# The loads of a and V begun from ScalarE's queue instead of SyncE's, in a Mamba-2 scan followed by a low-rank mixer

## The chip, the cores and the metric

The kernel runs on one core of one Trainium2 chip. The metric is the device time of one execution in microseconds (us). The engines of the core are named as the profile names them: PE (TensorE; PEld are its weight loads), DVE (VectorE), ACT (ScalarE), POOL (GpSimd) and SP (SyncE); SPq is the queue of SP, from which loads and stores are begun.

## The reference

Two blocks follow each other. The first is a chunked state-space scan over 4 batches, 8 heads, 768 steps, with head dimension 32 and state dimension 16; the second mixes its output along the sequence with two low-rank factors U and V and along the channels with two weight matrices.

```python
log_a = np.log(np.clip(a, 1e-06, 1.0))
for c in range(nc):                      # chunks of 32 steps
    cum = np.cumsum(la, axis=-1)
    L = np.exp(cum[:, :, :, None] - cum[:, :, None, :]) * causal
    CB = np.einsum('bhin,bhjn->bhij', Cc, Bc)
    y_intra = np.einsum('bhij,bhjd->bhid', CB * L, xc)
    y_inter = np.einsum('bhin,bhnd->bhid', Cc, state) * decay_to_i[:, :, :, None]
    y[:, :, sl] = y_intra + y_inter
    state = decay_full[:, :, None, None] * state + np.sum(Bx, axis=2)
...
h = xt @ U @ V                           # xt: (batch, 256, 768); U: 768 x 32; V: 32 x 768
u = x + h.transpose(0, 2, 1)
ch = np.maximum(u @ w_ch1, 0.0) @ w_ch2
return (u + ch).astype(np.float32)
```

U, V and the two weights come as 64-bit numbers and are turned into 32-bit ones on the chip from their integer words.

## The kernel before

The sequence is worked in blocks of 256 steps: 4 batches times 3 blocks make 12 pairs, numbered 0 to 11. For each pair the kernel loads x, B and C, scales B and C by the decays (tile BC), transposes them on PE (tiles T and Cm), forms the masked products (tile M), adds up the state (tiles S and Sm), and sums the outputs in PSUM (yT). For each batch the mixer then multiplies by U and V and by the weights.

The order of all work is written out by hand, as one list of words called PLAN. A word's first letters name a step and its numbers say on what: `A` the decays, `Q` the scaling of B and C, `V1.1.2` a transposition (not the load of V), `g` and `m`/`M` the products and their masks, `n` and `j` the two halves of the output inside a chunk, `s` and `u` the state, `y` the copy of yT, `c` and `C` the conversions of words, `v` the spreading of V over the partitions, `F` idle products on PE that are put ahead of the next step, `p`/`q`/`a` the low-rank part, `f`/`e`/`h`/`d`/`U` the channel part. Every engine works through its own instructions in the order of the list.

Loads are words too. `B`, `X` and `w` are held until the last DVE instruction ahead of them in the list is done. With a `Y` in front a load is begun as soon as its turn comes in SP's queue; with a `Z` in front it is begun from ACT's queue instead. No word of the list of before has a `Z`. `follow` picks the queue:

```python
if name[0] in "YZ":
    issuer[0] = nc.scalar if name[0] == "Z" else nc.sync
    early[name[1]](*at)
    issuer[0] = nc.sync
```

SP's queue therefore begins, in this order: a (ahead of the list, L186), U, B and C of pair 0, x of pair 0, pair 1, the B and C of pair 2, the four loads of V (`YV0`), the first half of the first weights (`w0`, held until `Q2.0`), x of pair 2, B and C of pair 3, and so on; L202 is the line of `begin`, through which all loads but a's go. The four loads of V bring one quarter of V's columns each to 32 partitions (48 KB each).

The first steps are these. ACT begins with the load of its function table (L182). PE runs idle products from the moment its identity matrix is there (L136), then transposes a (L343); DVE clips the result, ACT takes the logarithm (L349), and all decays come from that. V is needed by the conversion `C0`, and then by `v0`, which makes Vn (L880) and Vs (L890).

Of the kernel before, what the change touches and what calls it, by code (L numbers as in the profile page):

```python
# [32 lines left out]

PLAN = (
# [39 lines left out]
def kernel(  # L74
# [27 lines left out]
    nc = tc.nc  # L102
# [60 lines left out]
    class Kept:  # L163
# [6 lines left out]
        def __getattr__(self, name):  # L170
# [8 lines left out]
    vector = Kept(nc.vector)  # L179
    until = []  # L180

    nc.scalar.preload_act_table_set("natural_log_exp_and_others")  # L182


    a_sb = const.tile([NB * NH * NC // 2, 2, P], FP32)
    nc.sync.dma_start(  # L186
        out=a_sb,
        in_=a.rearrange("(g b) h (c s) -> g (b h c) s", g=2, s=P).rearrange(
            "g r s -> r g s"))

    x_sb, bc_sb = {}, {}
    pairs = [(b, q) for b in range(NB) for q in range(NPR)]
# [68 lines left out]
    U2, V2, w12, w22 = (w.bitcast(INT32) for w in (moe_U, moe_V, moe_w_ch1, moe_w_ch2))  # L261
# [721 lines left out]
```

## Time and profile before

| | |
|---|---|
| median of 3 runs | 224.49 us (224.32 to 224.66) |
| the profiled execution | 224.41 us |
| its span in the profile | 222.6 us |
| PE busy | 215.5 us, 97% of the span |
| DVE, ACT, POOL busy | 146.4, 108.7, 32.7 us |
| granted clock of PE | 0.999 |
| load of a, issue to landing | 2.0 us |
| loads of V, issue to landing | 2.8 us (median of four) |

The profile tells of one execution. A line of the timeline gives start, duration, engine, source line, operation, what is written from what, how often, and in brackets the idle time before it with what ended it. A line of the chain gives start, duration, engine, tile and source line of one piece of the chain of work that ended last.

### The profile page before, as it was taken

How to read it: one execution, taken by the hardware profiler on the slowest of the kernel's cores; microseconds unless marked ns; L12 is line 12 of the kernel's file. 1: busy time of each engine (PE TensorE's matmuls, PEld its weight loads, DVE VectorE, ACT ScalarE, POOL GpSimd, SP SyncE). 2: the span in 40 equal slices, each digit the busy share in tenths (PEclk: the TensorE clock that was granted, in tenths of full speed). 3: DMA queues.
4: the chain of work that ended last, by engine and by line, in shares of the span. 5: the costliest groups of instructions: out<-in, count | busy, mean ns of one | idle time of the engine just before them, and what ended most of it. 6: DMA issues, size and time to landing. Idle time of an engine off the chain costs nothing.

```text
span 222.6 us, 7025 instructions
## 1 busy us (share of the span) xinstructions
PE 215.5 (97%) x3022; PEld 182.2 (82%) x3022; DVE 146.4 (66%) x314; ACT 108.7 (49%) x251; POOL 32.7 (15%) x44
## 2 busy tenths in 40 slices
PE   7999999999999999999999999999999999999994
PEld 4666566665668888889999996788999999999993
DVE  4688498568657755737955736959863955674921
ACT  3334745675668075543444214476535455553510
POOL 3012223405577053000010100000000000000000
PEclk9999999999999999999999999999999999999999
DMA  6968888898633446100120010000000100101011
GB/s 102 129 98 144 138 158 189 187 281 113 134 47 71 84 57 91 37 24 28 27 71 27 3 49 27 3 3 3 0 27 1 47 0 27 47 0 50 6 43 50
DMA packets 69520, 14.59 MB, mean 66 GB/s; under 512 B 63792, under 2 KB 67696, under 8 KB 69488
## 3 DMA queue, kind: packets, MB, share of 16 engines
q1 hardware_dynamic: 69488, 14.13, 32.3%
q8 instruction: 24, 0.39, 0.8%
q14 instruction: 8, 0.07, 0.1%
HBM read 10.98 MB, written 3.15 MB: 63 GB/s over the span
## 4 chain that ended last, share of the span: by engine, by line
PE 89%; DVE 5%; DMA 2%; SPq 2%; ACT 1%; issue 1%; POOL 0%; POOLq 0%
PE x L790 31%; PE z L790 24%; PE y L790 12%; PE y L680 3%; PE x L522 2%; PE y L642 2%; PE w L482 2%; DMA bc<-in_B_dram 2%; DVE M L174 2%; PE w L707 2%; SPq L202 2%; PE w L556 1%; PE x L136 1%; PE z L522 1%; PE w L734 1%; PE w L136 1%
## 5 line engine op out<-in xcount | busy, mean ns | idle before, releaser
L790 PE MATMUL z<-u,w 128*128 128x384 f32 x144 | 33.6, 347 | 0.0
L790 PE MATMUL x<-u,w 128*128 128x384 f32 x144 | 32.7, 344 | 0.5 <-DVE u L174 0.3
L174 DVE SCALAR_TENSOR_TENSOR words<-words 128x768 fp32r<-128x768 f32 (+3 forms) x35 | 29.5, 846 | 1.4
L790 PEld LDWEIGHTS x<-u,w 128*128 128x128 f32 x144 | 24.8, 188 | 1.8 <-DVE u L174 0.7
L795 ACT ACTIVATE x<-x 128x384 f32<-128x384 f32 (+1 forms) x30 | 13.6, 454 | 25.1 <-PE x L790 18.2
L790 PEld LDWEIGHTS z<-u,w 128*128 128x128 f32 x144 | 24.1, 189 | 0.9
L790 PE MATMUL x<-w2c,words 128*128 128x256 f32 x112 | 22.3, 339 | 0.0
L795 ACT ACTIVATE z<-z 128x384 f32<-128x384 f32 (+1 forms) x27 | 12.6, 466 | 18.6 <-PE z L790 18.6
L790 PE MATMUL y<-w,words 128*128 128x256 f32 x144 | 19.8, 283 | 0.0
L790 PEld LDWEIGHTS x<-w2c,words 128*128 128x128 f32 x112 | 18.3, 189 | 1.5
L174 DVE SCALAR_TENSOR_TENSOR words<-x,words 128x384 fp32r<-128x384 f32 x24 | 13.3, 554 | 9.3 <-ACT words L825 9.2
L790 PEld LDWEIGHTS y<-w,words 128*128 128x128 f32 x144 | 18.8, 190 | 0.3
L583 POOL TENSOR_TENSOR Sm<-S,own 128x256 f32<-128x256 f32 (+1 forms) x12 | 7.6, 634 | 76.4 <-DVE S L174 48.0
L174 DVE SCALAR_TENSOR_TENSOR words<-z,words 128x384 fp32r<-128x384 f32 x24 | 13.2, 552 | 5.2 <-ACT words L825 5.1
L825 ACT ACTIVATE words<-z 128x384 fp32r<-128x384 f32 x24 | 11.7, 491 | 10.1 <-PE z L790 10.0
L825 ACT ACTIVATE words<-x 128x384 fp32r<-128x384 f32 x24 | 11.8, 493 | 5.3 <-PE x L790 5.0
L790 PE MATMUL x<-w,words 128*128 128x256 f32 x96 | 14.2, 285 | 0.0
L790 PEld LDWEIGHTS x<-w,words 128*128 128x128 f32 x96 | 12.9, 190 | 0.2
L680 PEld LDWEIGHTS y<-M,x 64*32 64x32 f32 x768 | 8.1, 105 | 5.7 <-issue 3.0
L174 DVE TENSOR_TENSOR BC<-bc,F 128x512 f32<-128x512 f32 (+2 forms) x18 | 9.4, 535 | 4.7 <-DMA bc<-in_B_dram 3.2
L680 PE MATMUL y<-M,x 64*32 64x64 f32 x768 | 12.0, 223 | 0.4 <-DVE settled L174 0.3
L174 DVE SCALAR_TENSOR_TENSOR S<-S,kept,w 128x64 f32<-128x64 f32 x40 | 11.2, 279 | 1.6
(149 smaller groups left out, 411.9 us busy)
## 6 DMA issues: line engine op xcount, KB each, us to landing
words<-in_moe_w_ch_dram SPq DMA_DIRECT2D x7, 512.0 KB, 5.0
x<-in_x_dram SPq DMA_DIRECT2D x24, 128.0 KB, 3.7
out_dram<-ytok SPq DMA_DIRECT2D x24, 128.0 KB, 1.7
bc<-in_B_dram SPq DMA_DIRECT2D x24, 64.0 KB, 3.3
bc<-in_C_dram SPq DMA_DIRECT2D x12, 128.0 KB, 3.4
words<-in_moe_w_ch_dram SPq DMA_DIRECT2D x2, 256.0 KB, 3.8
words<-in_moe_U_dram SPq DMA_DIRECT2D x1, 192.0 KB, 2.9
words<-in_moe_V_dram SPq DMA_DIRECT2D x4, 48.0 KB, 2.8
```

Source lines behind the costliest of these rows:

```text
L136: nc.tensor.matmul(out=t[:, :m * P].rearrange("p (m i) -> p m i", i=P), lhsT=ident, rhs=ident[:, None, :].to_broadcast([P, m, P]), start=T ...
L174: self.last = call(*args, **kwargs)
L202: op = issuer[0].dma_start(**kwargs)
L482: nc.tensor.transpose(out=tp[:, i, v], in_=s["BC"][:, i, c + v].rearrange("p h n -> p (h n)"), identity=ident)
L522: nc.tensor.matmul(out=s["g"][r][cols, c], lhsT=s["T"][rows, 0, c, cols], rhs=s["Cm"][rows, :, :, ts(2 * c + p, Q)].rearrange("r v t i -> ...
L583: nc.gpsimd.tensor_tensor(out=s["Sm"][:, sl], in0=s["S"][:, sl].rearrange("p i (s d) -> p i s d", s=2), in1=own2[:, b, 4 * q + sl.start:4 ...
L642: behind["first"].append(nc.tensor.matmul(out=channels(k)[r // 2][ts(r % 2, H), c, p], lhsT=own[ts(r, Q)], rhs=st[k]["T"][ts(r, Q), 1, :, ...
L680: product = nc.tensor.matmul(out=y[n][ts(i, Q), c, p], lhsT=x_sb[k][half, c, h], rhs=s["M"][half, h // 2, c, h % 2], start=fresh(k, n, [i] ...
L707: nc.tensor.transpose(out=t[:, c, g], in_=yT[b][:, g, ts(2 * q + c, P)], identity=ident)
L790: nc.tensor.matmul(out=t, lhsT=lhsT, rhs=rhs, start=start, stop=True, skip_group_check=True)
L795: nc.scalar.activation(t, t, AF.Copy, scale=1.0 + EPS)
L825: nc.scalar.activation(gs[j, m // 2][0][:, m % 2], t, AF.Relu, scale=NEAR)
```

## The change

The load of a is begun from ACT's queue, and the load of ACT's function table, which came first, now comes behind it. The word `YV0` becomes `ZV0`: V's four loads are begun from ACT's queue, at the place in ACT's order that the word has in the list, behind the two activations of `V1.1.2` and ahead of the copy of `V2.0.2`. Nothing else is changed.

```diff
-    'm0 Q1.1 V1.1.2 M0 u0 YX1 F5 F3 n0 YB2 g1 m1 YV0 Q2.0 w0 Q2.2 YX2 s1 i0 F3 V2.0.2 M1 j0 Q2.1 u1 '
+    'm0 Q1.1 V1.1.2 M0 u0 YX1 F5 F3 n0 YB2 g1 m1 ZV0 Q2.0 w0 Q2.2 YX2 s1 i0 F3 V2.0.2 M1 j0 Q2.1 u1 '
...
-    nc.scalar.preload_act_table_set("natural_log_exp_and_others")
-
-
     a_sb = const.tile([NB * NH * NC // 2, 2, P], FP32)
-    nc.sync.dma_start(
+    nc.scalar.dma_start(
         out=a_sb,
         in_=a.rearrange("(g b) h (c s) -> g (b h c) s", g=2, s=P).rearrange(
             "g r s -> r g s"))
+
+    nc.scalar.preload_act_table_set("natural_log_exp_and_others")
```

## The prediction

> **What bounds the kernel now.** I read the page first: span 222.6 us, the profiled run's own time 224.41, so 1.81 us lie outside the span; TensorE (PE) is busy 97%. By stages, PE is busy 22.11 us of the first 25 and 193.36 of the remaining 197.60, so a load can matter in the first 25 us only, or through a shift that these hand on to the end. Then I read the chain that ended last, in order of time, in that stage:
>
> ```profile
> 1.43 1.65 PE x L136 x2
> 3.08 0.33 PE w L343 x2
> ...
> 15.56 0.34 DVE M L174
> 15.90 0.04 SPq L202
> ...
> 15.99 1.39 SPq L202
> ...
> 19.61 4.09 DMA bc<-in_B_dram
> ...
> 23.72 0.69 DVE BC L174
> 24.41 0.10 DVE settled L174
> ...
> 24.55 0.46 PE y L680 x32
> ```
>
> Up to 15.9 us it is PE and VectorE (DVE); then it goes over SyncE's queue (SPq) and the load of pair 3's B, which ends at 23.7. This reads as if SP's queue were the limit. Whether it is depends on how much room the compute path beside it has, so next the timelines of SP, ACT, PEld (weight loads), DVE and PE, around the places of the change:
>
> ```profile
> 0.80 1.28 ACT L182 ACT_TABLE_LOAD   x1 [0.80 <-PEq L967]
> 0.81 0.38 SPq L186 DMA_DIRECT2D a_sb<-in_a_dram  x1
> 1.24 0.44 SPq L202 DMA_DIRECT2D words<-in_moe_U_dram  x1
> 2.82 0.29 PEld L343 LDWEIGHTS w<-ident,a_sb 96*128 96x128 f32 x2 [0.89 <-DMA a_sb<-in_a_dram]
> 2.88 0.37 PE L343 MATMUL w<-ident,a_sb 96*128 96x96 f32 x1
> 12.73 0.63 ACT L492 ACTIVATE Cm<-x,slot 128x128 f32<-128x128 f32 x2
> 13.46 1.98 SPq L202 DMA_DIRECT2D words<-in_moe_V_dram  x4
> 15.56 0.38 SPq L202 DMA_DIRECT2D words<-in_moe_w_ch_dram  x1
> 16.34 0.37 ACT L486 COPY T<-x 128x256 f32<-128x256 f32 x1 [2.98 <-PE x L482]
> 20.52 0.32 PE L556 MATMUL w<-x,BC 64*32 64x64 f32 x8 [0.26 <-DMA x<-in_x_dram]
> 21.07 0.35 PE L886 MATMUL y<-Vn,ident 32*32 32x192 f32 x2 [0.23 <-ACT Vn L880]
> 24.35 0.15 DVE L174 COPY settled<-slot 128x1 f32<-128x1 f32 x1
> 24.55 0.46 PE L680 MATMUL y<-M,x 64*32 64x64 f32 x32 [0.34 <-DVE settled L174]
> ```
>
> To be seen: a lands just as PE wants it; ACT sits idle for 2.98 us where V's loads are to go; and only two PE waits of the stage, 0.26 and 0.34 us, are ended by loads.
>
> **1. a, from SP to ACT.** Removed from SP: one issue; U begins at 0.81 in place of 1.24, and everything behind it moves up 0.43 us. Added to ACT: an issue of about the same 0.38 us, at 0.80, ahead of the table load. The table load then runs from about 1.2 to 2.5; the first activation that needs it starts at 3.98, so 1.5 us of cover hide it (gone, the cover would cost what the load overshoots, at most 0.4).
> The price is where a lands. Before, a (192 packets, 12 for each of the 16 DMA engines) has these engines nearly alone: between 1.80 and 2.35 us they move 193 packets at a 59.9% share, 27 ns each, 0.33 us an engine. U (768 packets, 48 an engine) follows: 430 packets between 2.5 and 3.0 at 94.8%, 17.6 ns each, 0.84 us an engine. After, both start at 0.8. If the engines take the two queues packet by packet, a's 12 packets have up to 12 of U's between them, 12 x 17.6 = 0.21 us; a little less, since U's packets came 1.13 us after its issue and a's 1.03. Bounds: 0 (a keeps its place ahead) and 0.84 (all of U goes first). Earlier it can hardly land, since both engines' first instructions start at 0.80 to 0.81; and earlier would bring nothing: the 384-column warm-up passes run 0.64 us apart further on (the two at L136 from 3.68 to 4.96), and the second one here, from 2.235, is through at 2.875, exactly when L343's first matmul starts. So a has 0.05 us of room (weight load at 2.82, matmul at 2.88). I take 0.18 later, the value of the interleaving, near the low bound because a's packets start about 0.1 ahead: 0.18 - 0.05 = +0.13 us for L343. Behind it PE works through fills in fixed order to 9.15, and DVE, PE and DVE in turn to 15.9, without a wait on a load: the 0.13 goes on.
> The trace of before has one load queue, so no row shows two at once. [...]
>
> **2. V, from SP to ACT.** Removed from SP: four issues, 1.98 us from 13.46 to 15.44. But SP's next load, w0, is held until the DVE product Q2.0 is done; that is the first of the two BC products of 14.94 and is finished at 15.2, set by PE and DVE. So w0 starts at 15.3 instead of 15.56, and SP gains 0.26, not 1.98. What follows (X2, B3, B5 and so on) comes 0.26 us earlier at least, up to some 0.6 when V's bytes are already out of the way.
> Added to ACT: four issues of 0.42 to 0.58, 1.85 us with their gaps taken as on SP, behind the two Cm activations (12.73 to 13.36) and ahead of the T copy of 16.34. 13.36 + 1.85 = 15.2, so 1.1 us of the 2.98 idle are left: nothing. What is queued behind them is that T copy, then the Cm's and the yT copies of 17.12; PE waits for each of them (L680 at 17.57 starts as yT is done). [...] V lands at 18.2 before, and DVE's first V conversion starts at 18.39 right behind the Cm of 17.68; earlier landing moves nothing.
>
> **3. What the earlier SP queue is worth.** Two PE waits. (a) 0.26 at 20.52 for X2's second half. With it gone PE is through with L556 earlier, and then stands longer at 21.07, for Vn: ACT makes Vn at 20.65 to 21.01 behind the yT copies of 20.11, which PE's own L680 releases. Worth 0. (b) 0.34 at 24.55 for "settled". This tiny DVE copy also has to wait for the 32 products of L680 at 23.76, the last of which ends at 24.22, and its semaphore comes at 24.32; the BC product that the load held up frees DVE at about 24.33. The two are level, so the load gives 0.02 us at most. The same at 28.64: DVE was held 0.32 us by a load at 27.50, but the M product there needs PE's L522, ending 28.58. Worth 0 to 0.04. I take -0.03 for all three.
> [...]
>
> **Sum.** 0.13 - 0.03 = +0.10 us on the profiled 224.41, so 224.51; the median of the three runs is 224.49, so about 224.6.
>
> **Rivals.**
> - Faster: the compute path has more room than the rows let me see (a level pair is a matter of hundredths, and inferred releasers can name the wrong one), and both waits fall away: -0.26 - 0.34 = -0.60, a not later: 223.9. For it: the chain as the profile draws it does run over SP and B3. Against: (a) and (b) above.
> - Slower, U ahead of a: with 0.84 us of U's packets in front, a lands 0.84 later, minus the 0.05 of room: +0.79, and all of it reaches the end: 225.3. It decides from a landing 0.5 us late, at about 3.3, on. For it: SP's and ACT's first issue start within 0.01 us. Against: half-way interleaving is likelier.
> - Slower, ACT held: if V's issues take over 0.745 us each (2.98 / 4), the T copy starts late; at 1.0 each (X2's first issue took 1.39), 1.0 us late: 225.5.
> - The move does nothing: ACT's issues serve in the same order as SP's did, a lands at 2.78: 224.5.
>
> **How the numbers follow.** A measurement of this kernel can tell about 0.2%, 0.45 us, from no change. Forecast (a later by up to 0.5, rest hidden) 0.54, nothing 0.04: together 0.58 within. U ahead of a 0.19, ACT held 0.08: 0.27 slower. Waits fall away 0.15: faster. The range runs from the faster rival to U ahead of a: 223.8 to 225.3; the forecast's own part is 224.4 to 224.9.
>
> **What would show it.** Right: L343's first weight load at 2.9 to 3.1; U's landing, 4.15 before, near 3.8; V's four issues on ACT done before 16.3 and the T copy not later than PE's L482; w0 at 15.3; PE's 0.26 at 20.52 gone and the 0.23 at 21.07 grown; "settled" at 24.3 to 24.6. Wrong: L343 at 2.82 with a shorter span (rival one), L343 after 3.3, or ACT's T copy behind V's issues.

## The result: 1.1 us slower, and the profile after

The changed kernel takes 225.49 us (median of 5 runs, 225.25 to 226.01) against 224.35 for the kernel before, measured beside it (5 runs, 223.81 to 224.66). The ratio over all runs is 1.0066, with a 95% interval of 1.0051 to 1.0080, which is 1.1 to 1.8 us; that of the medians alone, 1.0051, stands at the lower end. The profiled execution took 225.49 us, its span is 223.8.

The chain that ended last now starts with a load. The columns are start, duration, engine, tile and line (the lines of the new kernel are one lower than those of the old):

```profile
0.80 3.15 DMA a_sb<-in_a_dram
3.95 0.05 issue
4.00 0.58 PE w L342 x2
4.58 0.48 PE x L136 x2
...
21.93 0.26 ACT Vn L879
...
25.52 0.17 DVE settled L174
...
```

a takes 3.15 us from issue to landing, where it took 1.97; it lands at 3.95 instead of 2.78, and PE transposes it at 4.00 instead of 2.88. From there on the chain is PE, ACT and DVE only. SP and the load of pair 3's B, which stood in the chain before, are out of it. The timelines of ACT, SP, PEld and PE show the places of the change:

```profile
0.80 0.45 ACTq L183 DMA_DIRECT2D a_sb<-in_a_dram  x1
1.28 1.28 ACT L188 ACT_TABLE_LOAD   x1 [1.28 <-PEq L966]
0.81 0.43 SPq L201 DMA_DIRECT2D words<-in_moe_U_dram  x1
4.00 0.29 PEld L342 LDWEIGHTS w<-ident,a_sb 96*128 96x128 f32 x2 [2.07 <-DMA a_sb<-in_a_dram]
13.64 0.32 ACTq L201 DMA_DIRECT2D words<-in_moe_V_dram  x1
14.01 0.43 ACTq L201 DMA_DIRECT2D words<-in_moe_V_dram  x1
14.47 0.91 ACTq L201 DMA_DIRECT2D words<-in_moe_V_dram  x2
16.42 0.37 SPq L201 DMA_DIRECT2D words<-in_moe_w_ch_dram  x1
17.51 0.37 ACT L485 COPY T<-x 128x256 f32<-128x256 f32 x1 [2.98 <-PE x L481]
22.23 0.35 PE L885 MATMUL y<-Vn,ident 32*32 32x192 f32 x2 [0.57 <-ACT Vn L879]
25.73 0.46 PE L679 MATMUL y<-M,x 64*32 64x64 f32 x32 [0.34 <-DVE settled L174]
```

The shift is 1.12 us at a's transposition (4.00 against 2.88), 1.17 at ACT's T copy (17.51 against 16.34), 1.18 at the "settled" product (25.73 against 24.55), 1.2 over the span, and 1.14 in the medians. Between these two profiles it arises in one place and is handed on whole. The medians are less exact than that: against the 29 runs of before that stand beside the first experiments (224.16) the loss would be 1.33.

In the packets of the trace a's delay has three parts. Its first packet comes at 2.24 instead of 1.84 (0.41 later), although a was issued at the same moment. Its 192 packets take 0.96 us from the first to the last instead of 0.59 (0.37 more). And from the last packet to the landing 0.75 us pass instead of 0.36 (0.39 more). Together that is 1.17. The packets of the two loads are mixed: of U's 768, 190 start ahead of a's first, 500 between a's first and last and 78 behind; 227 packets of B of pair 0 lie there too.

### The profile page after: what moved, and what is told of

It reads as the page before. It is cut to its first block, busy times and chain, and to the rows that moved or that the text cites. A ratio compares the mean times of both kernels' runs of the same rounds, so it can differ in the third digit from the quotient of the medians.

```text
span 223.8 us, 7025 instructions
## 1 busy us (share of the span) xinstructions
PE 215.6 (96%) x3022; PEld 182.1 (81%) x3022; DVE 146.2 (65%) x314; ACT 108.6 (49%) x251; POOL 32.4 (14%) x44
## 3 DMA queue, kind: packets, MB, share of 16 engines
HBM read 10.98 MB, written 3.15 MB: 63 GB/s over the span
## 4 chain that ended last, share of the span: by engine, by line
PE 93%; DVE 3%; DMA 1%; ACT 1%; issue 0%
PE x L789 31%; PE z L789 24%; PE y L789 12%; PE y L679 4%; PE y L641 3%; PE x L521 3%; PE w L481 2%; PE w L706 2%; PE w L555 2%; DMA a_sb<-in_a_dram 1%; PE x L136 1%; PE z L521 1%; PE w L733 1%; PE w L751 1%; PE x L761 1%; PE w L741 1%
## 5 line engine op out<-in xcount | busy, mean ns | idle before, releaser
L824 ACT ACTIVATE words<-z 128x384 fp32r<-128x384 f32 x24 | 11.7, 490 | 10.2 <-PE z L789 10.0
```

Of the source, the lines that this page charges most:

```text
L824: nc.scalar.activation(gs[j, m // 2][0][:, m % 2], t, AF.Relu, scale=NEAR)
```

## The experiments

The theory (S): a's landing beside SP's first load is the whole difference. The rivals: V's loads on ACT cost or bring something (V); ACT's queue, or the table load behind a, is slow by itself (Q). The runs of before beside them have a median of 224.16 (29 runs) for V alone, a alone, U held back and the reverse, and of 224.13 (14 runs) for the other three.

**V alone on ACT's queue.**

```diff
-... g1 m1 YV0 Q2.0 w0 ...
+... g1 m1 ZV0 Q2.0 w0 ...
```

> Only V's four loads go to ACT's queue; a stays on SP, ahead of U. Theory S (the 1.1 us come from a's landing beside U's packets): a lands at 2.78 as before, L343's first weight load at 2.82, and the time is that of before, 224.35 within 0.3; w0 starts near 15.3, PE's 0.26 wait at 20.5 is gone and the wait for Vn has grown to about 0.5. Theory V (V's issues on ACT cost, or the earlier SP queue gives, part of it): the time differs from before by over 0.3 us, up (ACT's T copy of 16.34 late) or down.

Measured: 224.33 us (12 runs), ratio 1.0004 (0.9993 to 1.0014). Timelines of its SP, ACT and PE:

```profile
14.61 0.37 SPq L202 DMA_DIRECT2D words<-in_moe_w_ch_dram  x1
15.70 0.37 ACT L486 COPY T<-x 128x256 f32<-128x256 f32 x1 [2.98 <-PE x L482]
20.42 0.35 PE L886 MATMUL y<-Vn,ident 32*32 32x192 f32 x2 [0.41 <-ACT Vn L880]
23.86 0.46 PE L680 MATMUL y<-M,x 64*32 64x64 f32 x32 [0.34 <-DVE settled L174]
```

ACT still waits 2.98 us for PE ahead of the T copy, w0 is begun right behind Q2.0, the wait for X2 is gone, the wait for Vn has grown from 0.23 to 0.41, and the 0.34 at "settled" stands. V's move is worth nothing that these runs can tell, and the interval leaves it 0.3 us at most, so theory V falls. (This execution ran some 0.65 us ahead of that of before from 12 us on; the last section says why.)

**a alone on ACT's queue.**

```diff
-    nc.scalar.preload_act_table_set(...)
-    nc.sync.dma_start(out=a_sb, ...)
+    nc.scalar.dma_start(out=a_sb, ...)
+    nc.scalar.preload_act_table_set(...)
```

> Only a goes to ACT's queue, ahead of the table load; V stays on SP. Theory S: a lands at 3.95 as in the changed kernel, 1.1 to 1.2 us slower than before, 225.5. Theory V: less than the whole difference, since V's share is missing.

Measured: 225.44 us (4 runs), ratio 1.0061 (1.0042 to 1.0081); a lands at 3.97:

```profile
0.80 3.17 DMA a_sb<-in_a_dram
```

That is the time of the changed kernel within 0.05 us, so the whole loss is a's.

**U held back, a on ACT.** The changed kernel, but SP's first load waits for a short DVE instruction.

```diff
+    begun = vector.memset(ref, 0.0)
...
+            if name == "YU":
+                until[:] = [begun]
```

> The changed kernel, but U (SP's first load) is held until DVE's memset of ref is done, so that it starts at about 1.25 us, as it did behind a on SP; a is still on ACT, ahead of the table load. Theory S: a's packets have the DMA engines to themselves again, a lands at 2.75 to 2.9, and the time goes back to that of before, 224.4 within 0.3. Theory Q (ACT's queue itself, or its first load, or the moved table load is slow): a still lands at 3.3 or later, and the time stays at 225.0 or above.

Measured: 224.33 us (12 runs), ratio 1.0004 (0.9993 to 1.0015). Timelines of its ACT, SP and PEld:

```profile
0.80 0.39 ACTq L183 DMA_DIRECT2D a_sb<-in_a_dram  x1
1.24 0.42 SPq L201 DMA_DIRECT2D words<-in_moe_U_dram  x1
2.98 0.29 PEld L342 LDWEIGHTS w<-ident,a_sb 96*128 96x128 f32 x2 [1.04 <-DMA a_sb<-in_a_dram]
```

a is on ACT's queue and still ahead of the table load, and it lands at 2.94, its first packet at 1.83 as on SP. So neither ACT's queue nor the moved table load is slow by itself: theory Q falls, and the neighbour on the other queue is what it takes. This profile, the slowest of its 12 runs (224.71), has a second thing to show. The load of the second half of pair 2's x took 4.03 us to land, where it took 3.06 before, and PE stood 1.28 us for it:

```profile
17.41 4.03 DMA x<-in_x_dram
```

**U held back less.** The same, with the memset of `ones` in place of that of `ref`, so that U follows 0.29 us behind a.

> The changed kernel with U held only until DVE's memset of ones is done, so that it starts at about 1.1 us, some 0.3 behind a. Theory F (of two issues at the same time SP's load gets its descriptors first; whoever is issued clearly earlier goes first): a's first packet is at 1.83 to 1.9, a lands at 2.9 to 3.2, and the time is within 0.3 of before. Theory P (SP's queue has precedence even when it starts later): a's first packet is at 2.1 or later, a lands at 3.5 or later, 0.6 us or more over before.

Measured: 224.05 us (10 runs), ratio 1.0000 (0.9984 to 1.0015); a's first packet at 1.85, landing at 2.89. Timelines of its ACT, SP and PEld:

```profile
0.80 0.40 ACTq L183 DMA_DIRECT2D a_sb<-in_a_dram  x1
1.09 0.42 SPq L201 DMA_DIRECT2D words<-in_moe_U_dram  x1
2.93 0.29 PEld L342 LDWEIGHTS w<-ident,a_sb 96*128 96x128 f32 x2 [1.00 <-DMA a_sb<-in_a_dram]
```

A lead of 0.29 us is enough, as theory F had it.

**The reverse: a on SP, U on ACT, at the same moment.**

```diff
-    'YU0 c0 F3 YB0 A0 ...
+    'c0 F3 YB0 A0 ...
...
     nc.sync.dma_start(out=a_sb, ...)
+    issuer[0] = nc.scalar
+    load_u()
+    issuer[0] = nc.sync
     nc.scalar.preload_act_table_set(...)
```

> The reverse: a on SP as the first load, U on ACT ahead of the table load, both begun at about 0.8; V on SP. Theory S: what hurts is the sharing, whichever queue a is on: a lands late again, at 3.3 to 4.0, and the time is 0.5 to 1.2 us over before. Theory Q: a on SP lands at 2.8 and U on ACT lands late; the time is that of before, 224.4.

Measured: 224.57 us (10 runs), ratio 1.0013 (1.0000 to 1.0026). Timelines of its SP, ACT and PEld:

```profile
0.81 0.39 SPq L294 DMA_DIRECT2D a_sb<-in_a_dram  x1
0.80 0.46 ACTq L194 DMA_DIRECT2D words<-in_moe_U_dram  x1
3.28 0.29 PEld L345 LDWEIGHTS w<-ident,a_sb 96*128 96x128 f32 x2 [1.35 <-DMA a_sb<-in_a_dram]
```

Neither theory's number: a lands at 3.24, between the two. Its first packet is on time (1.84), and it is U on ACT that starts late (2.15). What is left is the sharing alone: a's packets take 0.80 us instead of 0.59 (0.21 more), and 0.59 instead of 0.36 pass from the last one to the landing (0.23 more). So the order of the two queues matters as well as the sharing.

**One queue, a behind U.**

```diff
-    'YU0 c0 F3 YB0 A0 ...
+    'c0 F3 YB0 A0 ...
...
+    load_u()
     nc.sync.dma_start(out=a_sb, ...)
     nc.scalar.preload_act_table_set(...)
```

> One queue only: U is SP's first load and a its second, at about 1.25; V on SP. Theory F: coming second is nearly all of it, a lands at 3.6 to 4.0 as in the changed kernel, and the time is 0.8 to 1.2 us over before. Theory I (two queues at once cost more than one behind the other, since the packets interleave): a lands clearly earlier than 3.95, at 3.4 or before, 0.6 us over before or less.

Measured: 225.70 us (4 runs), ratio 1.0070 (1.0054 to 1.0085). Its chain begins:

```profile
0.81 0.43 SPq L194
...
1.29 2.82 DMA a_sb<-in_a_dram
...
4.15 0.58 PE w L343 x2
```

a lands at 4.11, only 0.16 later than in the changed kernel, where it was issued 0.49 earlier on a queue of its own. Putting a on ACT beside U does nearly what putting it behind U on SP does.

**B instead of U beside a.**

```diff
-    'YU0 c0 F3 YB0 A0 ...
+    'YB0 YU0 c0 F3 A0 ...
```

> The changed kernel, but SP's first loads are B and C of pair 0 and U comes behind them; a is on ACT at 0.8. B has 1024 packets of 64 bytes in place of U's 768 of 256. Theory F (SP's load goes first, a second): a starts at 2.2 again and lands at 3.6 to 4.0, 0.8 to 1.2 us over before. Theory K (it is U's packets between a's that cost, packet by packet): B's are 10.9 ns each against 17.7, so that a lands earlier by some 0.1 to 0.4, at 3.5 to 3.8; if only the order counted it would not.

Measured: 225.05 us (5 runs), ratio 1.0042 (1.0028 to 1.0056). Its chain has a's load as:

```profile
0.80 2.89 DMA a_sb<-in_a_dram
```

a starts at 2.28 and lands at 3.69: second again, but 0.26 sooner than beside U. The gain lies in the packets (0.76 us from first to last instead of 0.96) and behind them (0.65 instead of 0.75). Between a's packets lie 673 of B's and 70 of C's here, in the changed kernel 500 of U's and 227 of B's. Their own time, shared out over 16 engines, is 0.51 and 0.71 us: 0.20 apart, as the two streams of a are. Both theories hold a part: a is put second, whatever the load beside it, and then pays for the neighbour's packets.

All nine kernels in one table, by a's landing:

| kernel | begun together with a or ahead of it | a's first packet | a lands | time |
|---|---|---|---|---|
| before | nothing | 1.84 | 2.78 | 224.16 |
| V alone | nothing | 1.82 | 2.86 | 224.33 |
| U 0.29 behind | nothing | 1.85 | 2.89 | 224.05 |
| U 0.44 behind | nothing | 1.83 | 2.94 | 224.33 |
| reverse | U on ACT | 1.84 | 3.24 | 224.57 |
| B beside | B on SP | 2.28 | 3.69 | 225.05 |
| changed | U on SP | 2.24 | 3.95 | 225.49 |
| a alone | U on SP | 2.23 | 3.97 | 225.44 |
| a behind U | U on SP, ahead | 2.61 | 4.11 | 225.70 |

The changed kernel was timed against a median of 224.35, the others against 224.16 or 224.13. Over the runs of before beside each kernel, the time grows by about 1.1 to 1.3 us for each us that a lands later than 2.9. Why it is more than 1 is not shown. PE's change of pace (last section) comes at 5.0 to 7.1 us in the first four profiles of the table and at 7.9 to 10.2 in the other five, and may be a part of it. None of the versions is faster than the kernel before beyond its interval.

## Why the prediction was wrong

**1, a's move: the step that failed.** The mechanism was seen and the path was right: a has 0.05 us of room, and what goes beyond it reaches the end whole (1.12 at PE, 1.14 in the medians). Its size was wrong. I took 0.18 us later, net +0.13, from the bounds 0 and 0.84; it was 1.17, outside the bounds. Three things were missing.
- I let a's packets start 0.1 us ahead of U's, from the rows of one queue. With two queues issued within 0.01 us, SP's load was served first in all four such kernels, and ACT's first packet came 0.30 to 0.38 us behind SP's, whichever load it was.
- I let one packet of U come between two of a's. In the reverse experiment, where a is first, the price came out, 0.21 us, but by luck: its trace has 255 of U's packets between a's, 16 for each engine and not 12. Second in line there are 727 of U's and B's, 45 for each engine, and a paid 0.37.
- I priced only the time up to a's last packet. The time from there to the landing grows too, by 0.23 to 0.39 us, and no step of the sum had it. Without its 0.39 the delay would be 0.78, inside the bounds. The upper one was none for another reason too: U's packets took 1.18 us from first to last before (2.37 to 3.56), not 0.84.

The trace shows that U's and a's packets are mixed, 500 of U's between a's first and last. How many an engine takes at a time is not shown, since the trace does not name a packet's engine; 12, 16 and 45 are shares of a count, worked out over 16 engines.

**The chances and the range.** I gave 0.54 to interleaving and 0.19 to U ahead of a. What happened lies between the two: U's load went first, but with only 190 of its 768 packets, and the rest was interleaved. The cost, +1.14, is over the +0.79 of the dearer one, and the range ended at 225.3, since its upper end was that price. The row that spoke for it, two first issues 0.01 us apart, deserved more: without any row of two queues at once there was no ground to call interleaving likelier.

**2, V's move: right.** V's issues took 0.32 to 0.44 each, even beside the Cm activations rather than behind them, and were done 2.1 us ahead of the T copy. w0 was begun at 16.42; less the 1.17 of shift that is 15.25, forecast 15.3. SP gained the 0.3, not the 1.98.

**3, what the earlier SP queue is worth: right.** The 0.26 at X2 is gone and the wait for Vn grew from 0.23 to 0.57; the 0.34 at "settled" stands, now with the chain to it over PE and DVE alone, as the level pair would have it. V alone gave 1.0004. The margin is small, though: with U held back, X2's second half came late and PE waited 1.28 us for it in the profiled execution, so a load of this stage can still set the time of a single run.

**The table load: right.** With U held back it runs behind a and costs nothing that 12 runs can tell. **U's landing: wrong.** Forecast at 3.8, it came at 4.33, 0.18 later than before, though issued 0.43 earlier; in the reverse, on ACT's queue, at 4.08. Beside a, the earlier issue brought U next to nothing.

## What to carry to other kernels

A load that the first step waits for wants to be the only one begun for its first 0.3 us (0.29 was enough here). A second queue did not give it a lane of its own (a landed at 3.95), while at the head of SP's queue it had the others 0.4 us behind it (2.78). When a small load is put beside a large one, price its start, its stream and the time from its last packet to the landing (0.41, 0.37 and 0.39 us here), all three, from a run that has two queues in it, or keep the whole range open. And a chain that runs over a load queue need not be limited by it: see what else the step behind it waits for.

## What the hardware showed that was not expected

Two loads issued within 0.01 us, one from SP and one from ACT, did not start together: SP's first packet came at 1.84 to 1.92 and ACT's at 2.15 to 2.28, in four kernels, with either load on either queue. With ACT's load issued 0.29 or 0.44 us ahead of SP's, its first packet came at 1.85 and 1.83. Why SP's load goes first in a tie is left open; no run began ACT's load ahead by more than 0.01 and less than 0.29 us.

PE doubles its pace somewhere in the first microseconds, and not at the same time in the nine profiles. A product with 384 columns follows the last by 640 ns before that point; the point lies between 5.0 (V alone) and 10.2 us (a alone), with 7.1 before and 8.0 in the changed kernel. The mean granted clock of the nine is 0.998 to 1.0 all the same, since the trace's records of the clock begin only at this point. The chain lines of two of them show it, first V alone, then a alone:

```profile
5.20 0.34 PE w L377 x2
```

```profile
9.85 0.56 PE z L391 x2
```

Before, the first of these took 0.64 us (at 5.16) and the second 0.33 (at 8.27). That is why V alone ran ahead of the kernel before in its profile, with a span of 221.9, while the medians agree, and probably a part of why the runs of before spread from 223.56 to 224.67. It is not all of such a spread: U held back has the point at 6.2 us and still a span of 222.9, with the wait for x told above. What sets the point is not shown. That it moves is seen from kernel to kernel, one profile each, by 5 us between the earliest and the latest.
